# Turning the gate logits of an attention and mixture-of-experts kernel to token rows: 24 small products replaced by three transposes

## The chip, the cores and the metric

The kernel runs on one core of a Trainium2 chip. The metric is the device time of one execution in microseconds; for the kernel before, three runs are known. The engines are called PE (TensorE matmuls), PEld (its weight loads), DVE (VectorE), ACT (ScalarE), POOL (GpSimd) and SP (the queue that issues the transfers).

## The reference

Attention with a window and sink tokens gives 1536 rows of 512 numbers; a dense two-layer block follows, and then eight experts weighted by a gate. The change touches the gate only:

```python
def _moe2_ref(x, w_gate, w1, w2):
    N, D = x.shape                      # 1536, 512
    E = w_gate.shape[1]                 # 8
    logits = x @ w_gate
    logits = logits - logits.max()
    P = np.exp(logits)
    for _ in range(8):
        P /= P.sum(1, keepdims=True) + 1e-09
        P /= P.sum(0, keepdims=True) + 1e-09
        P *= N / E
    out = np.zeros((N, D), dtype=np.float32)
    for e in range(E):
        h = np.maximum(x @ w1[e], 0.0)
        ye = h @ w2[e]
        out += P[:, e:e + 1] * ye
    return out
```

## The kernel before

Attention is computed first. From then on PE works through units. A unit `u` is a pair `(p, c)`: 256 hidden features `p` of a layer and one half `c` of the tokens (768 of 1536). Its first matrix product is done in seven block products `i = 0..6` (`product`, L686) of six matmuls with 384 columns each, because every operand is held as a high and a low part. Products 0, 2, 4 and 5 gather in a PSUM tile `pa`, products 1, 3 and 6 in `pb`. `post` takes them away: ACT copies `pa` to a tile `m` after products 0, 2 and 4 (L693), DVE adds `pb` to it (L699, L708), and ACT and DVE write the high and low part of `h` (L655, L656). A later product into the same `pa` has to wait until that copy has read it.

The second layer of unit `u - 1` is spread over unit `u` as tiles `y` (`l2tile`, L733: six matmuls of 512 columns, three PSUM buffers). They are added to the sum `acc` by DVE (L743, L745) or, for the first feature pair of the experts, copied by ACT (L741).

The order of all this is written out by hand. Step `s = 7u + i` is product `i` of unit `u`, and small jobs hang on steps in three lists: `pre` (before the product), `mid` (after `post`) and `aft` (after the `y` tiles of the step). Each engine takes its instructions in the order in which they were written; a waiting instruction holds up all that stands behind it on its engine.

The gate's logits are computed in units 17 to 19. `gate_split` (POOL, step 112) writes the gate weights as 96 columns `gs`: eight with the high parts, eight with the low parts, zeros. `logits(c, half)` (steps 122, 126, 130, 134) multiplies them with a quarter of the tokens, 384 columns, into the PSUM tile `lps`; ACT copies the 16 rows that matter to a tile `m` (L767). The logits then lie as 16 rows by 384 tokens. `logits_out` (three `mid` steps after each) turns 128 tokens at a time to token rows, and adds the high and low part on the way, with one fp32 product with the 16x8 matrix `pick` (L773), which PE runs as two matmuls. So there are four quarters, 12 products and 24 matmuls. After every third, ACT copies 24 columns to `pr`, 128 tokens by 12 groups by 8 experts (L776).

Then `max_rows`, `max_flip` and `max_exp` find the largest logit and take the exponential, and eight rounds follow of `sink_rows` (five DVE instructions, L793 to L797), `sink_sum` (a product with ones on PE, `cps`, L801) and `sink_cols` (four DVE instructions, L804 to L807). A round takes three steps: `sink_sum` stands two steps behind `sink_rows`, and `sink_cols` one step behind that. Meanwhile `x_fast` prepares the experts' input for the second half of the tokens, on ACT (L267), DVE (L270) and, for two subtractions of 768 columns, POOL (L231); POOL also splits the coming weights (L174, L175).

Of the kernel before, what the change touches and what calls it, by code (L numbers as in the profile page):

```python
# [7 lines left out]
F32 = mybir.dt.float32  # L8
# [3 lines left out]
AF = mybir.ActivationFunctionType  # L12
ALU = mybir.AluOpType
# [3 lines left out]
P = 128  # L17
# [23 lines left out]
def attention_moe_sinkhorn_kernel(  # L41
# [14 lines left out]
    nc = tc.nc  # L56
    B, H, S, D = q.shape
    NTOK, DM = out.shape
    NE, _, FE = w1.shape
    KD = DM // P  # L60
    NQ = S // P
    TH = S // 2
    TQ = S // P
# [6 lines left out]
    pools = {}  # L70
    for nm, bufs in (("const", 1), ("xp", 1), ("stage", 3), ("conv", 2), ("convs", 1), ("wg1", 2), ("wg2", 2), ("ws", 1)):
        pools[nm] = ctx.enter_context(tc.tile_pool(name=nm, bufs=bufs))
    const, xp = pools["const"], pools["xp"]

    ident = const.tile([P, P], F32, name="ident")
# [4 lines left out]
    wide = const.tile([P, 5], F32, name="wide")  # L80
    flag = const.tile([P, 1], I32, name="flag")
    gate = const.tile([P, KD, NE], F32, name="gate")
    pick = const.tile([2 * NE, NE], F32, name="pick")
    X = [xp.tile([P, 7, 2, 2, TH], F32R, name="x0"), None]
    acc = [None, xp.tile([P, KD * S], F32, name="acc1")]

# [235 lines left out]

    def load_gate():
        nc.sync.dma_start(out=gate, in_=w_gate.rearrange("(k p) e -> p k e", p=P))
        nc.vector.tensor_tensor(pick, ident[0:2 * NE, 0:NE], ident[0:2 * NE, NE:2 * NE], op=ALU.add)

    def attention(first):
        with ExitStack() as es:
# [171 lines left out]
            for m in range(NU + 2):  # L500
# [34 lines left out]
                if m == 0:  # L535
                    load_pair(2, "qk")
                    load_pair(1, "v")
                    load_gate()
# [75 lines left out]
    def moe(again):  # L614
        with ExitStack() as es:
            def pool(nm, bufs, **kw):
                return es.enter_context(tc.tile_pool(name=nm, bufs=bufs, reuse_waits="tile", **kw))

            hp, tp, ep = (pool(nm, n, side="right") for nm, n in (("hp", 6), ("mt", 4), ("ep", 3)))
# [53 lines left out]
            unit = {}  # L673
# [76 lines left out]
            mb = [None]  # L750
# [8 lines left out]
            def logits(c, half):  # L759
                g = unit["g"]  # L760
                ps = ps_m.tile([96, TH], F32, tag="m", name="lps")
                seq = [(i, j, k) for i, j in (((0, 0), (1, 2)), ((3, 0), (0, 0), (6, 2)))[half] for k in range(2)]
                seq = [(i, a, j, k) for a in range(2) for i, j, k in seq]
                for n, (i, a, j, k) in enumerate(seq):
                    nc.tensor.matmul(ps, lhsT=g[:, j + k], rhs=X[c][:, i, a, k], start=(n == 0), stop=(n == len(seq) - 1))  # L765
                l = tp.tile([P, TH], F32, tag="m", name="m")
                nc.scalar.activation(l[0:2 * NE], ps[0:2 * NE], AF.Copy)  # L767
                unit["l"] = l

            def logits_out(c, half, t):  # L770
                if t == 0:
                    mb[0] = ps_m.tile([P, TQ // 2, NE], F32, tag="m", name="lpt")
                nc.tensor.matmul(mb[0][:, t], lhsT=unit["l"][0:2 * NE, t * P:(t + 1) * P], rhs=pick)  # L773
                if t == TQ // 2 - 1:
                    r = c * TQ + half * (TQ // 2)
                    nc.scalar.activation(pr[:, r:r + TQ // 2], mb[0], AF.Copy)  # L776

            def max_rows():
                nc.vector.tensor_reduce(lmax[:, 0:1], pr.rearrange("p t e -> p (t e)"), axis=AX.X, op=ALU.max)
# [46 lines left out]
            pre, mid, aft = {}, {}, {}  # L826

            def at(d, i, fn, *args):
                d.setdefault(i, []).append(lambda: fn(*args))
# [41 lines left out]
            i = 7 * U + 10  # L871
            for c in range(2):
                for half in range(2):
                    at(mid, i, logits, c, half)
                    for t in range(TQ // 2):
                        at(mid, i + 1 + t, logits_out, c, half, t)
                    i += 4
            at(pre, i, max_rows)
            at(mid, i + 1, max_flip)
            at(pre, i + 2, max_exp)  # L880
# [5 lines left out]
            i = max(i + 4, 14 * (NPX + NPE))  # L886
# [48 lines left out]
            for t in tiles:  # L935
                t()

    first = moe(False)
    attention(first)
    masks[0] = None  # L940
    for _ in first:
        pass
    with tc.If(nc.values_load(flag[0:1, 0:1], min_val=0, max_val=4 * P) > 0):
        general_attention()
        for _ in moe(True):
            pass
# [31 lines left out]
```

## Time and profile before

| | |
|---|---|
| runs of the kernel before | 1443.67, 1445.56, 1445.78 us, median 1445.56 |
| profiled execution, its own time | 1445.62 us |
| its span, first to last instruction | 1443.8 us |
| PE busy | 1411.7 us, 98% |
| DVE, POOL, ACT busy | 61%, 49%, 36% |
| chain that ended last | PE 88%, DVE 7%, ACT 2%, POOL 2% |

The page gives the busy time of each engine, and the chain of work that ended last by engine and line. The timeline of one engine gives the start of each group of like instructions. A matmul's busy time overlaps the next one's, so what a group costs PE is the distance from its start to the next group's start, not its busy time.

### The profile page before, as it was taken

The numbers are of one execution on the slowest core, as the hardware profiler recorded it, in microseconds if no ns is written. First come the engines' busy times: TensorE is split into PE (matmuls) and PEld (weight loads), VectorE is DVE, ScalarE is ACT, GpSimd is POOL, SyncE is SP. The second block draws the span as 40 slices with busy tenths as digits, with TensorE's granted clock in tenths as the row PEclk, the third lists the DMA queues.
The fourth block names the chain that finished last, engine by engine and source line by source line (L and its number), as shares of the span: only waits on it lengthen the run. The fifth ranks groups of instructions, "written<-read, shape, count | busy, mean of one in ns | idle before, by whom it ended". The sixth has DMA issues, their size and how long they took to land.

```text
span 1443.8 us, 19897 instructions
## 1 busy us (share of the span) xinstructions
PE 1411.7 (98%) x7531; PEld 1279.7 (89%) x7531; DVE 881.2 (61%) x1626; ACT 524.9 (36%) x1151; POOL 714.5 (49%) x843
## 2 busy tenths in 40 slices
PE   7899999999999999999999999999999999999998
PEld 5788889999988888898899889889889889988987
DVE  6877677777784485555555555555555555555544
ACT  5777677667543312222222222222222222222221
POOL 4789745446583446543345444335544334544410
PEclk9999999999999999999999999999999999999999
DMA  7342112112010000110001001000101000100002
GB/s 155 87 87 39 45 59 74 59 63 84 30 59 15 30 30 30 44 44 30 30 30 42 32 30 45 30 30 30 44 30 44 30 30 30 43 31 30 15 1 90
DMA packets 76633, 64.30 MB, mean 45 GB/s; under 512 B 40176, under 2 KB 64752, under 8 KB 76528
## 3 DMA queue, kind: packets, MB, share of 16 engines
q1 hardware_dynamic: 76240, 62.94, 14.7%
q8 instruction: 61, 1.00, 0.3%
q14 instruction: 44, 0.36, 0.1%
q10 hardware_dynamic: 288, 0.00, 0.0%
HBM read 59.79 MB, written 3.15 MB: 44 GB/s over the span
## 4 chain that ended last, share of the span: by engine, by line
PE 88%; DVE 7%; ACT 2%; POOL 2%; issue 1%; DMA 0%; DVEq 0%; ACTq 0%; POOLq 0%
PE y L733 43%; PE pa L686 21%; PE pb L686 16%; PE po L468 3%; PE sps L414 2%; PE xps L450 1%; DVE x L270 1%; PE tps L397 1%; DVE acc L743 1%; PE lps L765 0%; DVE ptB L458 0%; DVE cg L162 0%; ACT h L665 0%; DVE h L667 0%; POOL wg L175 0%
## 5 line engine op out<-in xcount | busy, mean ns | idle before, releaser
L733 PE MATMUL y<-w2s,h 128*128 128x512 f32 x2304 | 584.5, 394 | 0.0
L733 PEld LDWEIGHTS y<-w2s,h 128*128 128x128 f32 x2304 | 427.2, 188 | 72.6
L745 DVE SCALAR_TENSOR_TENSOR acc<-y,pr,acc 128x512 f32<-128x512 f32 x336 | 252.3, 751 | 325.5 <-PE y L733 324.1
L686 PE MATMUL pa<-x,wg 128*128 128x384 f32 x1920 | 387.8, 336 | 2.2 <-ACT m L693 2.0
L686 PEld LDWEIGHTS pa<-x,wg 128*128 128x128 f32 x1920 | 342.2, 188 | 26.1 <-ACT m L693 2.5
L686 PE MATMUL pb<-x,wg 128*128 128x384 f32 x1440 | 290.0, 335 | 3.1 <-DVE h L667 2.7
L693 ACT ACTIVATE m<-pa 128x384 f32<-128x384 f32 x240 | 117.7, 490 | 436.6 <-PE pa L686 436.3
L686 PEld LDWEIGHTS pb<-x,wg 128*128 128x128 f32 x1440 | 253.6, 188 | 10.3 <-DVE h L667 2.0
L174 POOL TENSOR_SCALAR w2s<-raw 128x512 fp32r<-128x512 f32 x64 | 49.0, 765 | 389.8 <-PE y L733 389.8
L655 ACT ACTIVATE h<-m 128x384 fp32r<-128x384 f32 x192 | 100.9, 526 | 295.6 <-DVE m L708 252.2
L733 PE MATMUL y<-h,w2s 128*128 128x384 f32 x768 | 146.9, 335 | 2.8 <-ACT cs L143 1.9
L656 DVE SCALAR_TENSOR_TENSOR h<-m,h 128x384 fp32r<-128x384 f32 x192 | 139.4, 726 | 1.0 <-ACT h L655 0.8
L733 PEld LDWEIGHTS y<-h,w2s 128*128 128x128 f32 x768 | 134.2, 188 | 3.7 <-POOL w2s L174 2.3
L175 POOL TENSOR_TENSOR wg<-raw,wg 128x512 fp32r<-128x512 f32 (+1 forms) x96 | 114.1, 1188 | 8.0
L743 DVE TENSOR_TENSOR acc<-y,acc 128x384 f32<-128x384 f32 (+1 forms) x148 | 84.2, 584 | 39.0 <-PE y L733 38.5
L174 POOL TENSOR_SCALAR wg<-raw 128x512 fp32r<-128x512 f32 (+1 forms) x96 | 54.6, 569 | 97.7 <-PE pa L686 82.8
L708 DVE TENSOR_TENSOR m<-m,pb 128x384 f32<-128x384 f32 x128 | 70.3, 549 | 28.8 <-PE pb L686 28.8
L699 DVE TENSOR_TENSOR m<-m,pb 128x384 f32<-128x384 f32 x80 | 44.2, 553 | 71.3 <-ACT m L693 71.1
L175 POOL TENSOR_TENSOR w2s<-raw,w2s 128x512 fp32r<-128x512 f32 x64 | 84.5, 1320 | 5.3
L175 POOL TENSOR_TENSOR wg<-ws,wg 128x512 fp32r<-128x512 f32 x40 | 54.0, 1350 | 3.3
L655 ACT ACTIVATE h<-pa 128x384 fp32r<-128x384 f32 x64 | 31.5, 492 | 47.7 <-PE pa L686 47.6
L414 PE MATMUL sps<-tk,tq 64*128 64x288 f32 (+2 forms) x288 | 38.3, 358 | 4.3 <-DVE nmax L420 4.3
(141 smaller groups left out, 1298.9 us busy)
## 6 DMA issues: line engine op xcount, KB each, us to landing
raw<-in_moe_w_dram SPq DMA_DIRECT2D x64, 512.0 KB, 3.4
raw<-in_moe_w_in_dram SPq DMA_DIRECT2D x16, 512.0 KB, 3.9
raw<-in_moe_w_out_dram SPq DMA_DIRECT2D x16, 512.0 KB, 3.2
qn<-in_q_dram SPq DMA_DIRECT2D x16, 192.0 KB, 4.0
kn<-in_k_dram SPq DMA_DIRECT2D x16, 192.0 KB, 4.4
vn<-in_v_dram SPq DMA_DIRECT2D x16, 192.0 KB, 3.3
out_dram<-acc SPq DMA_DIRECT2D x12, 256.0 KB, 2.1
par<-in_n_sink_dram ACTq DMA_DIRECT2D x1, 1.0 KB, 2.9
```

The lines of the kernel that those rows point to most:

```text
L174: nc.gpsimd.tensor_scalar(hi, r, 1.0, 1.0, op0=ALU.mult, op1=ALU.mult)
L175: nc.gpsimd.tensor_tensor(lo, r, r32(hi), op=ALU.subtract)
L414: nc.tensor.matmul(ps[:, :b - a], lhsT=x[r, t * P:(t + 1) * P], rhs=y[r, a:b], start=(w == 0), stop=(w == 2))
L655: nc.scalar.activation(h[:, 0], c, AF.Relu)
L656: later.append(lambda: nc.vector.scalar_tensor_tensor(h[:, 1], c, 0.0, r32(h[:, 0]), op0=ALU.max, op1=ALU.subtract))
L686: nc.tensor.matmul(d, lhsT=w[:, s, k], rhs=x[:, t, k], start=(n == 0 and i in (0, 1, 3)), stop=(n == len(seq) - 1), skip_group_check=i in ...
L693: nc.scalar.activation(m, a, AF.Copy)
L699: nc.vector.tensor_tensor(m, m, b, op=ALU.add)
L708: nc.vector.tensor_tensor(c, m, b, op=ALU.add)
L733: nc.tensor.matmul(y, lhsT=lhsT, rhs=rhs, start=(i == 0), stop=(i == len(seq) - 1))
L743: nc.vector.tensor_tensor(o, y, o, op=ALU.add)
L745: nc.vector.scalar_tensor_tensor(o, y, pr[:, c * TQ + tt, e:e + 1], o, op0=ALU.mult, op1=ALU.add)
```

## The change

The tile `pick`, and the DVE instruction that made it, are gone. The four quarters' 16 rows are no longer copied to a tile each: the first takes a buffer of the pool `convw`, which the weights of the layer before have left, POOL fills 384 of its columns with zeros, and quarter `i` is copied by ACT to partitions `32 i` to `32 i + 15`. One step after the last quarter three transposes of 128x128 (the names `lpt<-ident,cg`) turn all of it to token rows; ACT copies the high parts to `pr`, and DVE adds the low parts. `max_rows` and all that follows of the gate stands one step earlier; `weigh_first` stays at step 168.

```diff
-    pick = const.tile([2 * NE, NE], F32, name="pick")
...
-        nc.vector.tensor_tensor(pick, ident[0:2 * NE, 0:NE], ident[0:2 * NE, NE:2 * NE], op=ALU.add)
...
-                l = tp.tile([P, TH], F32, tag="m", name="m")
-                nc.scalar.activation(l[0:2 * NE], ps[0:2 * NE], AF.Copy)
-                unit["l"] = l
-
-            def logits_out(c, half, t):
-                if t == 0:
-                    mb[0] = ps_m.tile([P, TQ // 2, NE], F32, tag="m", name="lpt")
-                nc.tensor.matmul(mb[0][:, t], lhsT=unit["l"][0:2 * NE, t * P:(t + 1) * P], rhs=pick)
-                if t == TQ // 2 - 1:
-                    r = c * TQ + half * (TQ // 2)
-                    nc.scalar.activation(pr[:, r:r + TQ // 2], mb[0], AF.Copy)
+                i = 2 * c + half
+                if i == 0:
+                    unit["l"] = pools["convw"].tile([P, DM], F32, tag="g", name="cg")
+                    nc.gpsimd.memset(unit["l"][:, 0:TH], 0.0)
+                nc.scalar.activation(unit["l"][32 * i:32 * i + 2 * NE, 0:TH], ps[0:2 * NE], AF.Copy)
+
+            def logits_out():
+                lt = ps_m.tile([P, TQ // 2, 4, 32], F32, tag="m", name="lpt")
+                l = unit.pop("l")
+                for t in range(TQ // 2):
+                    nc.tensor.transpose(lt[:, t].rearrange("p i r -> p (i r)"), l[:, t * P:(t + 1) * P], ident)
+                o = pr.rearrange("p (i t) e -> p t i e", i=4)
+                nc.scalar.activation(o, lt[:, :, :, 0:NE], AF.Copy)
+                nc.vector.tensor_tensor(o, lt[:, :, :, NE:2 * NE], o, op=ALU.add)
...
                     at(mid, i, logits, c, half)
-                    for t in range(TQ // 2):
-                        at(mid, i + 1 + t, logits_out, c, half, t)
                     i += 4
+            i -= 1
+            at(mid, i - 2, logits_out)
             at(pre, i, max_rows)
```

On PE, at the last quarter (steps 134 to 138), the rows before:

```order
L765 MATMUL lps<-x_2382,gs 96x384 x12
L733 MATMUL y<-w2s,h 128x512 x6
L686 MATMUL pa<-x_2382,wg_5016 128x384 x6
L773 MATMUL lpt<-pick,m 128x8
L686 MATMUL pb<-x_2382,wg_5065 128x384 x6
L773 MATMUL lpt<-pick,m 128x8
L733 MATMUL y<-w2s,h 128x512 x12
```

and now:

```order
L763 MATMUL lps<-x_2380,gs 96x384 x12
L731 MATMUL y<-w2s,h 128x512 x6
L684 MATMUL pa<-x_2380,wg_5014 128x384 x6
L774 MATMUL lpt<-ident,cg 128x128 x3
L684 MATMUL pb<-x_2380,wg_5063 128x384 x6
L731 MATMUL y<-w2s,h 128x512 x12
```

The small products between the large ones are gone (a row here is one product, which the trace shows as two matmuls), and three transposes stand together.

On POOL, at the first quarter (step 122; `acc` are the two subtractions of `x_fast`), the rows now:

```order
L173 TENSOR_SCALAR w2s<-raw 128x512
L174 TENSOR_TENSOR w2s<-raw,w2s 128x512
L230 TENSOR_TENSOR acc_90<-acc_90 128x2x384
L767 MEMSET cg 128x384
L230 TENSOR_TENSOR acc_90<-acc_90 128x2x384
```

Before, the two subtractions stood together; the filling with zeros now stands between them.

On ACT, from the same step on, with what each row waits for, the rows before:

```order
L693 ACTIVATE m<-pa 128x384 [waits PE_49,Activation_49]
L767 ACTIVATE m<-lps 16x384 [waits PE_49,Activation_49]
L741 ACTIVATE acc_2383<-y 128x512 [waits PE_49] x2
L267 ACTIVATE x_2382<-acc_91 128x768 [waits DVE_49]
L693 ACTIVATE m<-pa 128x384 [waits PE_49,Activation_49]
```

and now:

```order
L691 ACTIVATE m<-pa 128x384 [waits PE_49,Activation_49]
L768 ACTIVATE cg<-lps 16x384 [waits PE_49,Pool_49]
L739 ACTIVATE acc_2381<-y 128x512 [waits PE_49] x2
L266 ACTIVATE x_2380<-acc_90 128x768 [waits DVE_49]
L691 ACTIVATE m<-pa 128x384 [waits PE_49,Activation_49]
```

The copy of the first quarter's logits now also waits for POOL, with the same four instructions behind it.

## Rows read from the trace of the kernel before

**Rows 1.** The page, busy time and share of each engine.

```profile
PE 1411.7 (98%) x7531; PEld 1279.7 (89%) x7531; DVE 881.2 (61%) x1626; ACT 524.9 (36%) x1151; POOL 714.5 (49%) x843
```

**Rows 2.** Timeline of PE at the logits: start us, us, engine line op.

```profile
436.05 1.22 PE L686 MATMUL pa<-x,wg 128*128 128x384 f32 x6
437.21 0.38 PE L773 MATMUL lpt<-pick,m 16*128 16x8 f32 x2
...
444.93 1.22 PE L686 MATMUL pa<-x,wg 128*128 128x384 f32 x6
...
474.02 0.38 PE L773 MATMUL lpt<-pick,m 16*128 16x8 f32 x2
```

**Rows 3.** Timeline of PE after the gate, with large products alone.

```profile
552.94 1.21 PE L686 MATMUL pa<-x,wg 128*128 128x384 f32 x6
553.99 1.20 PE L686 MATMUL pb<-x,wg 128*128 128x384 f32 x6
555.03 1.55 PE L733 MATMUL y<-w2s,h 128*128 128x512 f32 x6
556.41 1.21 PE L686 MATMUL pa<-x,wg 128*128 128x384 f32 x6
```

**Rows 4.** Tile lpt: weight loads (ns min/median/max), and idle time before them.

```profile
L773 PEld LDWEIGHTS lpt<-pick,m x24: 181/182/184, 437.2 to 480.0; 16*128 16x128 f32 x24
...
  issue: 3.0, 12
```

**Rows 5.** Timeline of PE at the transpose that the kernel has already.

```profile
484.17 1.21 PE L686 MATMUL pb<-x,wg 128*128 128x384 f32 x6
485.21 0.27 PE L785 MATMUL mps<-ident,m 128*128 128x128 f32 x1
...
486.72 1.20 PE L686 MATMUL pa<-x,wg 128*128 128x384 f32 x6
```

**Rows 6.** Timeline of PE at a product with ones of the eight rounds.

```profile
541.61 1.20 PE L686 MATMUL pb<-x,wg 128*128 128x384 f32 x6
542.65 0.28 PE L801 MATMUL cps<-cpart,ones 128*128 128x8 f32 x2
...
545.62 1.23 PE L686 MATMUL pa<-x,wg 128*128 128x384 f32 x6
```

**Rows 7.** Timeline of POOL at the first quarter; in brackets the idle time before and its releaser.

```profile
434.53 3.63 POOL L231 TENSOR_TENSOR acc<-acc 128x768 f32<-128x768 f32 x2 [4.96 <-DVE x L270]
```

**Rows 8.** Tile gs: the zero filling of another tile by POOL.

```profile
L755 POOL MEMSET gs<- x1: 412/412/412, 418.5 to 418.5; 128x384 f32 x1
```

**Rows 9.** Timeline of ACT at the first quarter, and at the last quarter's copy.

```profile
433.55 0.48 ACT L767 ACTIVATE m<-lps 16x384 f32<-16x384 f32 x1 [0.81 <-PE lps L765]
...
436.25 0.60 ACT L741 ACTIVATE acc<-y 128x512 f32<-128x512 f32 x1 [0.77 <-PE y L733]
436.75 0.83 ACT L267 ACTIVATE x<-acc 128x768 fp32r<-128x768 f32 x1
437.48 0.48 ACT L693 ACTIVATE m<-pa 128x384 f32<-128x384 f32 x1
...
471.75 0.48 ACT L767 ACTIVATE m<-lps 16x384 f32<-16x384 f32 x1 [1.00 <-PE lps L765]
```

**Rows 10.** Timeline of PE during the eight rounds: the groups it waited for.

```profile
500.59 1.32 PE L686 MATMUL pb<-x,wg 128*128 128x384 f32 x6 [0.29 <-DVE m L699]
...
522.38 0.39 PE L801 MATMUL cps<-cpart,ones 128*128 128x8 f32 x2 [0.42 <-DVE cpart L797]
...
524.39 1.28 PE L686 MATMUL pa<-x,wg 128*128 128x384 f32 x6 [0.16 <-ACT m L693]
```

**Rows 11.** Timeline of DVE: first and last of one round's nine instructions.

```profile
504.15 0.15 DVE L804 TENSOR_SCALAR cinv<-cps 128x8 f32<-128x8 f32 x1
...
507.61 0.36 DVE L797 TENSOR_REDUCE cpart<-pr 128x8 f32<-128x96 f32 x1
```

**Rows 12.** Timeline of DVE ahead of max_rows.

```profile
480.60 0.55 DVE L699 TENSOR_TENSOR m<-m,pb 128x384 f32<-128x384 f32 x1 [9.26 <-ACT m L693]
```

## The prediction

> **What bounds the kernel now.** I read the page first. PE is busy for 98% of the span and no other engine for more than 61% [rows 1], so what PE is spared counts, unless PE then waits for something else. Next I read PE's timeline at the logits, to see what the small products cost in their place. Large products alone follow each other at fixed distances: 1.05 us from a `pa` or `pb` group to the next, 1.38 us from a `y` group to the next [rows 3]. Whatever lies beyond these distances is the price of what stands between. Last I read ACT and POOL at the first quarter, because the change lets an ACT instruction wait for POOL there, and DVE in the eight rounds, which the change moves by a step.
>
> **Removed: 12 products, 24 matmuls.** From the `pa` of step 123 to the `pa` of step 126 PE takes 444.93 - 436.05 = 8.88 us [rows 2]. In it lie three groups of 1.05, three of 1.38 and three small products. The large groups alone would take 3 x (1.05 + 1.38) = 7.29, so a small product costs 0.53 us. The other three quarters give the same within 0.02 us, by the same reckoning. Twelve cost 12 x 0.53 = 6.4 us, all on PE's path, since PE runs without a gap here. The busy times hide that: two matmuls of eight columns look like 0.38 us, most of it overlapped. The trace shows where the price comes from: each of the 12 pairs has some 0.25 us in which the weight load stands idle for "issue" (3.0 us in 12 cases), and then two loads of 0.18 us [rows 4].
>
> Removing the four ACT copies to `pr` and the one small DVE instruction that makes `pick` gains nothing: neither is what PE waits for.
>
> **Added on PE: three transposes.** One transpose of the same shape is there already: from `pb` to `pa` around it PE takes 486.72 - 484.17 = 2.55 us, against 1.05 + 1.38 = 2.43 without [rows 5]. That is 0.12 to 0.13 us each, 0.4 us for three. They wait for the last quarter's copy, which starts at 471.75 and takes 0.48 us [rows 9], while their place is where a small product starts at 474.02 [rows 2]: 1.8 us to spare, so no wait. The Trainium skill ("TensorE: Matmul & The Clock Gate", Part 4) speaks against cheap transposes: about 0.275 us each in a kernel. By that figure the three would cost 0.8 us, and the sum would come out 0.4 us worse; the row above has the measured price among neighbours, so I keep 0.4.
>
> **Added on ACT and DVE behind the transposes.** ACT copies to `pr` and DVE adds. DVE stood idle for 9.26 us before its instruction at 480.60 [rows 12], so the addition, and `max_rows` behind it, lie in that gap. Cost on PE's path: none. Were the cover gone, it would be one DVE instruction of at most the 0.55 us that a wider one takes there.
>
> **Added: a wait of ACT for POOL.** The zero filling stands on POOL between the two subtractions, as its order shows, and the first of these starts only at 434.53, released by DVE; the two take 3.63 us, so the first ends at about 436.35 [rows 7]. A filling of the same 128x384 takes 0.41 us [rows 8]. So the first quarter's copy, which ran at 433.55 [rows 9], now starts at about 436.8. Behind it on ACT stand two copies of `y` (0.50 us from start to start), one of `x` (0.73) and the copy of `pa` after product 4 [rows 9]. That copy then ends at 436.8 + 0.48 + 2 x 0.50 + 0.73 + 0.48 = 439.5, where it ended at 437.96 before. Product 5 writes into the same `pa` and has to wait for it. Without the small product it would start at 436.05 + 1.05 + 1.38 = 438.5. **PE waits 1.0 us.** Nothing worse follows: the next `y` groups have three buffers, the addition on DVE behind that copy (0.55 us) ends two PE groups before product 6 needs it, and ACT, idle before several rows here, catches up within the unit. Bounds: 0 if the filling came early, 1.5 if ACT's spacing is looser than these rows. The later three quarters wait for PE alone, as before.
>
> **Moved: `max_rows` and the eight rounds, one step earlier.** No instruction is added, but each round's nine DVE instructions, 3.8 us while POOL works beside them (504.15 to 507.97) [rows 11], meet other neighbours. Before, PE waited 0.29 + 0.42 + 0.16 = 0.87 us for this stage [rows 10]. Now other rounds stand ahead of the additions that free `pb` and of `h`; one of them, at step 146, stands right ahead of the low part of `h` that PE needs two steps on. I take the same total, so 0; the ends are a gain of 0.9, all of the old waits, and a loss of 2.1, two groups of 1.05 us by which a late round could hold PE. `weigh_first` stays where it was, so the rounds' earlier end moves nothing behind them. SP issues the same transfers.
>
> **The sum.** -6.4 + 0.4 + 1.0 + 0 = -5.0 us. The profiled execution took 1445.62 us, its span 1443.8 with 1.8 around it; that is 0.06 above the median of the runs. So I forecast **1440.6 us**, 0.35% less. A measurement of this kernel can tell about 0.2%, 2.9 us, from no change: below 1442.7 counts as faster.
>
> **Rivals.**
>
> *The wait for POOL isn't felt, or the old waits vanish.* If PE does not wait at product 5, the time is 1439.6; with the 0.87 us of the rounds gone as well, 1438.7. For it: PE has few waits anywhere in this stage. Against: the chain of ACT instructions above has no slack in its sum. 15%.
>
> *The moved rounds cost two more waits* of 1.05 us: 1442.7. For it: a round takes DVE 3.8 us beside POOL, while PE needs only a few groups for three steps, and PE did wait for such a round at 522.38 [rows 10]. Against: just three short waits in eight rounds before. 11%.
>
> *The small products cost only what like ones cost.* The product with ones has two matmuls of eight columns too, and from its `pb` to the `pa` behind it PE takes 4.01 us against 1.05 + 2 x 1.38 = 3.81 [rows 6], 0.2 us for the pair. If the other 0.33 us at `lpt` were not its own but a cost of the place that the transposes or the wait inherit, the change would save 12 x 0.2 = 2.4, and the sum would be -2.4 + 0.4 + 1.0 = -1.0: 1444.6, no change that can be told. The Trainium skill says that a weight load's time goes by its columns and not its rows ("TensorE: Matmul & The Clock Gate", LDWEIGHTS), by which a 16-row operand should cost what a 128-row one costs. The loads agree, 182 ns here [rows 4]; the idle 0.25 us ahead of them does not, and it stands at `lpt` alone. 8%.
>
> *Slower: the rounds fall behind in every step.* If the new places let each of the eight rounds end after PE has reached its product with ones, PE waits about one group, 1.05 us, in each: 8.4 us, against the 0.87 us that go. The sum is -5.0 + 8.4 - 0.9 = +2.5: 1448.1. It decides from about 0.7 us for each round on, where the gain is gone. Against: rounds and products move together and keep their distance of two steps, and DVE is busy for 61% of the span [rows 1]. 4%.
>
> **How the numbers follow.** The forecast keeps 62%, with 1439.8 to 1441.6 as its own range, which takes in a wait between 0.2 and 1.5 us and rounds that differ by half a microsecond. The range to hold 8 times in 10 reaches from the first rival's lower part to beyond the second, 1438.2 to 1443.8; outside lie the third and fourth (12%) and what is unknown. Faster by over 0.2%: 62 + 15 + about half of the second rival, 82%. Within 0.2%: the rest of the second and the third, 14%. Slower: 4%.
>
> **What would show it.** In the changed profile PE should have no group between large products at the first three quarters, with distances of 1.05 and 1.38 us; `lpt` should be three matmuls costing 0.4 us together; ACT's first copy of logits should start near 436.8 after a wait for POOL; and PE should show one wait of about 1 us for ACT's `m` near 438.5. In the eight rounds PE's waits should add up to around 0.9 us. I am wrong if the span from 436 to the first round shrinks by less than 4 us, if PE's waits in the rounds exceed 3 us, or if the time comes back later, for instance as PE waiting for POOL's weights.

## The result and the profile after

The changed kernel takes **1430.81 us** (median of 4 runs, 1428.6 to 1432.42); the kernel before took 1444.62 beside it (4 runs, 1441.36 to 1445.78). The ratio is 0.991, with a 95% interval of 0.9898 to 0.9922. It is faster, as forecast, but by nearly three times the 5.0 us forecast, and it lies below the range. The profiled execution took 1428.6 us, with a span of 1426.8.

The page, busy time by engine, after:

```profile
PE 1393.6 (98%) x7510; PEld 1273.4 (89%) x7510; DVE 884.1 (62%) x1626; ACT 523.8 (37%) x1148; POOL 714.1 (50%) x844
```

PE is busy for 18.1 us less than in [rows 1], with 21 instructions fewer. 21 small matmuls can't be 18 us, so other matmuls must have become shorter. To find them I took the starts of PE's products (a `pa` or `pb` group is one step's product, and both kernels issue the same 560) and compared the two kernels at the same five steps, 51, 101, 121, 181 and 551. Timeline of PE, before (start us, us, engine line op):

```profile
270.95 1.20 PE L686 MATMUL pa<-x,wg 128*128 128x384 f32 x6
...
381.58 1.20 PE L686 MATMUL pb<-x,wg 128*128 128x384 f32 x6
...
429.79 1.21 PE L686 MATMUL pa<-x,wg 128*128 128x384 f32 x6
...
581.79 1.21 PE L686 MATMUL pb<-x,wg 128*128 128x384 f32 x6
...
1408.27 1.21 PE L686 MATMUL pa<-x,wg 128*128 128x384 f32 x6
```

and after:

```profile
267.63 1.22 PE L684 MATMUL pa<-x,wg 128*128 128x384 f32 x6
...
379.33 1.21 PE L684 MATMUL pb<-x,wg 128*128 128x384 f32 x6
...
427.65 1.21 PE L684 MATMUL pa<-x,wg 128*128 128x384 f32 x6
...
572.39 1.21 PE L684 MATMUL pb<-x,wg 128*128 128x384 f32 x6
...
1391.48 1.21 PE L684 MATMUL pa<-x,wg 128*128 128x384 f32 x6
```

| stretch (us) | before | after | difference |
|---|---|---|---|
| start to step 51 (attention, first units) | 270.95 | 267.63 | -3.3 |
| 51 to 101 (dense layer) | 110.63 | 111.70 | +1.1 |
| 101 to 121 | 48.21 | 48.32 | +0.1 |
| 121 to 181 (gate, with the edit) | 152.00 | 144.74 | -7.3 |
| 181 to 551 (experts) | 826.48 | 819.09 | -7.4 |
| 551 to the end of the span | 35.53 | 35.32 | -0.2 |

The first row says nothing of the edit. `e4_fill_early`, `e15_noacc_d32` and `e13_rounds_old`, described below, run the changed kernel's instructions at its addresses up to step 51, and reach it at 271.95, 269.30 and 272.37 us. One cause is the granted clock: from 120 to 148 us it is 0.94 before and 1.00 after (column PEclk, third from the right, of the windows view; before first):

```profile
120.00:148.00 28.00, 26.27 (x200) 23.25 (x197) 19.25 (x65) 20.21 (x65) 23.48 (x34) 0.94 0.07 15
```

```profile
120.00:148.00 28.00, 25.30 (x198) 22.38 (x195) 18.91 (x62) 19.28 (x60) 23.61 (x39) 1.00 0.07 16
```

The 0.94 is a mean: from about 142.1 to 145.5 us the clock stood at 0.50, the lower of its two levels (1.2 GHz), and otherwise at the upper one (2.4 GHz). Just before, up to 140.79 us, PE had waited 1.19 us for DVE. Fifteen matmuls of 128x384 took 3.65 us from 141.76 on, and fifteen like them 2.20 us from 145.59 on, so this stay explains about 1.5 of the 3.3 us; the rest stays open. Because single runs differ by such amounts ahead of step 51, what follows goes by stretches behind it.

The rest adds up to -13.7 us, and the medians differ by 13.8. Only half of that stands where the code was edited. The other half is in the experts, where neither instructions nor order changed and PE waits for nothing in either kernel. Timeline of PE there, before and after:

```profile
1203.57 1.55 PE L733 MATMUL y<-w2s,h 128*128 128x512 f32 x6
1204.95 1.21 PE L686 MATMUL pa<-x,wg 128*128 128x384 f32 x6
```

```profile
1204.11 1.53 PE L731 MATMUL y<-w2s,h 128*128 128x512 f32 x6
1205.48 1.21 PE L684 MATMUL pa<-x,wg 128*128 128x384 f32 x6
```

A `y` group of six matmuls takes PE 1.37 us instead of 1.38 to 1.39, start to start. Added up from start to start, the 317 `y` groups of this stretch take 433.32 us instead of 439.44, the 211 `pa` groups 220.15 instead of 221.46, and the 159 `pb` groups 165.6 in both: that is the 7.4 us. In the dense layer it goes the other way: `pa` (303.38) to `y` (304.44) takes 1.06 after, where [rows 3] and the dense layer before (302.15 to 303.19) show 1.04 to 1.05.

```profile
302.15 1.20 PE L686 MATMUL pa<-x,wg 128*128 128x384 f32 x6
303.19 1.20 PE L686 MATMUL pb<-x,wg 128*128 128x384 f32 x6
```

```profile
303.38 1.22 PE L684 MATMUL pa<-x,wg 128*128 128x384 f32 x6
304.44 1.22 PE L731 MATMUL y<-h,w2s 128*128 128x384 f32 x6
```

What differs all over the program is where tiles lie. `pick` took 32 bytes of every partition. Without it, each tile allocated behind it at the lower end of SBUF (`x`, `acc`, `raw`, `cg`, `wg1`, `wg2`, `ws`, `pr`) lies 32 bytes lower: the first `x` at 18624 instead of 18656, `acc` at 61632 instead of 61664, by the allocation of the two built programs. The tiles at the upper end (`w2s`, `h`, `m`, `e`, `wg3`) stay. Below, the *difference* is the upper addresses minus the lower ones, modulo 128 bytes: 0 before, 32 after. The 128 is a way of counting; no run moved tiles by 128 bytes alone to see whether that changes nothing.

### The profile page after: what moved, and what is told of

It is laid out like the page before. It is cut to its first block, busy times and chain, and to the rows that moved or that the text cites. A ratio compares the mean times of both kernels' runs of the same rounds, so it can differ in the third digit from the quotient of the medians.

```text
span 1426.8 us, 19856 instructions
## 1 busy us (share of the span) xinstructions
PE 1393.6 (98%) x7510; PEld 1273.4 (89%) x7510; DVE 884.1 (62%) x1626; ACT 523.8 (37%) x1148; POOL 714.1 (50%) x844
## 4 chain that ended last, share of the span: by engine, by line
PE 88%; DVE 7%; ACT 2%; POOL 1%; issue 1%; DMA 0%; DVEq 0%; POOLq 0%; ACTq 0%
PE y L731 43%; PE pa L684 22%; PE pb L684 16%; PE po L466 3%; PE sps L412 2%; PE xps L448 1%; DVE x L269 1%; PE tps L395 1%; DVE acc L741 1%; DVE ptB L456 0%; DVE h L665 0%; ACT h L663 0%; DVE cg L161 0%; PE lps L763 0%; DVE cs L159 0%
## 5 line engine op out<-in xcount | busy, mean ns | idle before, releaser
L731 PE MATMUL y<-w2s,h 128*128 128x512 f32 x2304 | 576.3, 390 | 0.0
```

Source lines behind the costliest of these rows:

```text
L731: nc.tensor.matmul(y, lhsT=lhsT, rhs=rhs, start=(i == 0), stop=(i == len(seq) - 1))
```

## The experiments

The theory: the experts' gain comes from the addresses, and the edit's own work is worth about what was forecast. The rival: it comes from the edit's order and waits, which reach further than the sum said.

**Addresses put back, and moved alone.** `e1_pad_after` is the changed kernel with a dead tile in the place of `pick` (difference 0). `e2_pad_before` is the kernel before with a second one (96).

```diff
+    const.tile([2 * NE, NE], F32, name="pad")
```

> The changed kernel with an unused tile of 32 bytes per partition in the place of pick, so that every tile stands at the address it had before the change (x, acc, the weights of the first layer at 32 modulo 64 bytes); the instructions are those of the changed kernel. Theory A (addresses): the 32 bytes that pick gave up moved the tiles behind it, and that made the y groups of the experts quicker (1.39 to 1.37 us) and the groups of the dense layer slower (1.04 to 1.06). Then this kernel has the old distances again and takes about 1437 us, near my forecast of 1440.6. Theory B (the gate's own instructions made the rest quicker, or the runs differ by chance): 1431 us and y groups of 1.37.

> The kernel before with 32 unused bytes more behind pick, so that x, acc and the first layer's weights stand at 0 modulo 64 bytes as in the changed kernel; the instructions are those of before. Theory A: y groups of the experts at 1.37 us, dense layer at 1.06, and about 1444.6 - 7.8 + 1.7 = 1438.5 us. Theory B: 1444.6 us and 1.39.

`e1_pad_after` took 1439.98 us (5 runs) against 1446.12 of the kernel before (14 runs), a ratio of 0.9951 (0.9932 to 0.9971); `e2_pad_before` 1442.91, a ratio of 0.9988 (0.9974 to 1.0002), not told apart from no change. In `e1_pad_after` the experts are slow again, from 573.06 to 1399.55 or 826.49 us, and the `y` group takes 1.39:

```profile
573.06 1.21 PE L685 MATMUL pb<-x,wg 128*128 128x384 f32 x6
...
1210.48 1.55 PE L732 MATMUL y<-w2s,h 128*128 128x512 f32 x6
1211.87 1.21 PE L685 MATMUL pa<-x,wg 128*128 128x384 f32 x6
...
1399.55 1.20 PE L685 MATMUL pa<-x,wg 128*128 128x384 f32 x6
```

So the experts' gain is the addresses' and not the order's; the rival falls. The gate stretch is 145.75 here, against 152.00 before at the same addresses: **the edit itself gives 6.25 us**. In `e2_pad_before` the experts take 823.68 and the dense layer 111.83 (before 110.63). The 1438.5 us that theory A gave for it were missed: its `y` groups do fall to 434.17 us in all, but its `pa` and `pb` groups rise from 387.0 to 389.5, so another shift is no gain of the same size.

**Both ends moved.** `e3_right` moves the upper tiles of the changed kernel by 32 bytes too, so that the difference is 0 at new places; `e8_d64` moves them by 96 (difference 64; the tile has 24 columns instead of `NE`).

```diff
+            pool("rpad", 1, side="right").tile([P, NE], F32, name="rpad")
```

> The changed kernel with 32 unused bytes at the other end of SBUF, so that w2s, h, m and e stand at 0 modulo 64 bytes too, like all else. If what counts is each tile's own place in 64 bytes, at least as fast as the changed kernel, 1431 us or less, and y groups of 1.37 or less. If what counts is whether the two ends agree, the state of before is back in this respect (both were at 32): y groups of 1.39 and about 1437 us. Theory B: 1431 us.

> The changed kernel with 96 unused bytes at the other end of SBUF: the two ends then differ by 64 modulo 128 bytes, after 0 (e1, e3: y 1.39, dense layer 1.04), 32 (the changed kernel: 1.37, 1.06) and 96 (e2: 1.37, 1.06). If only the difference modulo 64 counts, as 64-byte lines would have it, the distances of e1 and e3 come back, 1.39 and 1.04, and about 1438 us; if it counts modulo 128, another pair of distances.

`e3_right`: 1437.31 us, a ratio of 0.9938 (0.9917 to 0.9959), experts 826.48, `y` group 1.39:

```profile
1211.41 1.55 PE L732 MATMUL y<-w2s,h 128*128 128x512 f32 x6
1212.80 1.21 PE L685 MATMUL pa<-x,wg 128*128 128x384 f32 x6
```

The relation between the two ends counts, not the place of either, as far as this shift of both by 32 bytes shows. In the traces that share a difference the experts' stretch repeats to the hundredth: 826.48 or 826.49 at 0 (before, `e1_pad_after`, `e3_right`, `e14_noacc_d0`), 819.09 at 32 (after, `e4_fill_early`, `e13_rounds_old`, `e15_noacc_d32`). So one trace is enough to tell such stretches apart. `e8_d64`: 1432.13 in one run, experts 819.80. So it isn't a matter of 64 bytes either: 0 and 64 differ by 6.7 us. By differences of 0, 32, 64 and 96 (in bytes moved, upper end against lower: 0, +32, -64, -32) the experts take 826.48, 819.09, 819.80 and 823.68 us. The time that PE spends in the `y` matmuls of the whole program is, before and after (groups of PE's lines; columns: busy us and mean ns of one, idle us before):

```profile
L733 PE MATMUL y<-w2s,h 128*128 128x512 f32 x2304 | 584.5, 394 | 0.0
```

```profile
L731 PE MATMUL y<-w2s,h 128*128 128x512 f32 x2304 | 576.3, 390 | 0.0
```

In `e8_d64` it is 578.2 us.

**The filling with zeros earlier.** `e4_fill_early` leaves everything of the change but fills one step before the first quarter, ahead of the subtractions.

```diff
+            def fill_logits():
+                unit["l"] = pools["convw"].tile([P, DM], F32, tag="g", name="cg")
+                nc.gpsimd.memset(unit["l"][:, 0:TH], 0.0)
...
+            at(aft, i - 1, fill_logits)
```

> The changed kernel with the zero filling one step earlier, ahead of both subtractions on POOL, which is idle there. PE's wait for the copy m near 437 (0.8 us; 0.96 by the distance of the groups) goes and nothing else changes: 0.8 to 1.0 us less than the changed kernel, about 1430. If that wait only hid another one behind it, no difference.

The filling runs at 431.67 and PE no longer waits (timeline of PE):

```profile
438.17 1.21 PE L684 MATMUL pa<-x,wg 128*128 128x384 f32 x6
439.21 1.53 PE L731 MATMUL y<-w2s,h 128*128 128x512 f32 x6
440.58 1.21 PE L684 MATMUL pa<-x,wg 128*128 128x384 f32 x6
```

The gate stretch falls from 144.74 to 143.69, by 1.05 us. In the total this can't be told: 1432.22 us (4 runs), a ratio of 0.9894 (0.9865 to 0.9922) to the kernel before. It is a better version by the stretch alone.

**The rounds at their old step.** `e13_rounds_old` keeps the products and transposes of the change but puts the rounds back.

```diff
-            i -= 1
-            at(mid, i - 2, logits_out)
+            at(mid, i - 3, logits_out)
```

> The changed kernel with max_rows and the eight rounds back at their old steps (one later); the transposes stay where they are. My forecast had the move at 0, with ends of a gain of 0.9 and a loss of 2.1 us. If the move took PE's waits in the rounds away, they come back here: 0.9 us by the profile's brackets (up to 1.5 by the distances of the groups), and the stretch from the first logits to the end of the rounds is longer by that. If the waits went because the small products went, no wait here either.

It took 1434.82 us in one run. The gate stretch becomes 146.18, 1.44 us longer, and two waits for DVE are back. The changed kernel has a single wait of PE from 420 to 575 us, the one for ACT at the first quarter (waits of PE: total us, times, longest):

```profile
PE pa L684 <- ACT m L691: 0.8, 1, 0.8
```

The two waits in the timeline of PE of `e13_rounds_old`, and between them the same groups without a wait (511.77 to 514.42):

```profile
495.95 1.52 PE L731 MATMUL y<-w2s,h 128*128 128x512 f32 x6
497.80 1.31 PE L684 MATMUL pb<-x,wg 128*128 128x384 f32 x6 [0.32 <-DVE m L697]
...
511.77 1.21 PE L684 MATMUL pa<-x,wg 128*128 128x384 f32 x6
...
514.42 1.22 PE L684 MATMUL pb<-x,wg 128*128 128x384 f32 x6
...
517.89 1.21 PE L684 MATMUL pb<-x,wg 128*128 128x384 f32 x6
519.57 0.39 PE L802 MATMUL cps<-cpart,ones 128*128 128x8 f32 x2 [0.48 <-DVE cpart L798]
...
521.59 1.28 PE L684 MATMUL pa<-x,wg 128*128 128x384 f32 x6
```

The brackets show 0.32 and 0.48 us of idle time, but the distances show more. From `y` to `pb` at the first wait PE takes 1.85 us where 1.37 is usual, so 0.48. At the second it takes 3.70 us from a product over `cps` and `y` to the next product, against 2.65, so 1.05. Together these are 1.5 us, about the 1.44 of the stretch. A bracket begins where the last matmul ends. It leaves out the overlap that is lost (the `y` group at 495.95 is busy for 1.52 us, and the next group usually starts after 1.37) and the slower groups behind the wait.

**Which tiles meet.** From `e1_pad_after` (difference 0), one set of tiles at a time is moved by 96 bytes, which is 32 the other way modulo 128, with a dead tile of 24 columns ahead and one of 8 behind. The tiles behind both dead tiles then move by 128 bytes, and keep their place only by the count modulo 128. The sets are `acc`, `x`, and `wg1` with `wg2` at the lower end; `w2s`, `h`, `m` with `e`, and `wg3` at the upper. The edit for `w2s` as an example:

```diff
+            pool("rpad0", 1, side="right").tile([P, 24], F32, name="rpad0")
...
+            pool("rpad1", 1, side="right").tile([P, 8], F32, name="rpad1")
```

> The changed kernel with all tiles at their old addresses as in e1, but the two tiles acc alone moved by 32 bytes down modulo 128 (padding before and behind them). If the quicker y groups come from DVE's reading and writing of acc beside PE's reading of w2s and h at the other end of SBUF, the y groups of the experts go to 1.37 us here and the rest stays at the old distances (dense layer 1.04). If acc has no part in it, all distances are those of e1: 1.39 and 1.04.

> As e5, but with the two tiles x moved alone, and acc at its old place. If PE's own reading of x is what meets w2s, h or wg3, the distances of y (1.39) or of the dense layer's groups (1.04) change here: to 1.37, or to 1.06. If not: 1.39 and 1.04.

> As e5, but with the weight tiles wg1 and wg2 of the first layer moved alone. If it is PE's weight loads of the next product groups (wg) during the last matmuls of a y group (which stream w2s) that cost, y groups go to 1.37 us here, and the dense layer's groups perhaps to 1.06. If not: 1.39 and 1.04.

> The changed kernel with all tiles at the old addresses as in e1, and the tiles w2s alone moved by 32 bytes up modulo 128. w2s is what PE streams in the experts' second layer, beside weight loads from h. If the pair w2s and h sets the y distance, it changes here and in e10 (from 1.39 to 1.37), while the changed kernel, which kept both together, could not have gained by it. If it is w2s against everything at the other end (x, wg, acc), y goes to 1.37 here as in the changed kernel, and the first layer's groups stay at 1.04.

> As e9 with the tiles h alone moved. y at 1.37 if h is what counts (PE loads it as weights, ACT and DVE write it); 1.39 if not.

> As e9 with the tiles m and e alone moved, which PE never reads: ACT and DVE write and read them. If PE's distances depend only on what PE reads, 1.39 and 1.04 as in e1. If the other engines' traffic counts, as e5 (acc alone: first-layer groups 1.06 in place of 1.04) has it, a change here too.

> As e9 with the tiles wg3 alone moved: the weights of products 3 and 6 (in pb), which lie at the other end from x and were apart from it in the changed kernel. If that pair counts, the distances from pb groups change here; the y distance of 1.39 stays.

| moved | time, one run | experts 181 to 551 | of it `y` | of it `pa` and `pb` | dense 51 to 101 |
|---|---|---|---|---|---|
| nothing (`e1_pad_after`) | 1439.98 (median) | 826.49 | 439.4 | 387.0 | 110.62 |
| `acc` (e5) | 1437.65 | 827.91 | 436.8 | 391.1 | 111.27 |
| `x` (e6) | 1442.55 | 827.35 | 436.7 | 390.7 | 111.46 |
| `wg1`, `wg2` (e7) | 1438.19 | 826.85 | 437.0 | 389.8 | 111.28 |
| `w2s` (e9) | 1446.11 | 832.49 | 443.7 | 388.8 | 111.82 |
| `h` (e10) | 1442.02 | 830.00 | 442.6 | 387.4 | 111.98 |
| `m`, `e` (e11) | 1446.57 | 831.07 | 442.0 | 389.0 | 111.81 |
| `wg3` (e12) | 1438.86 | 828.25 | 439.2 | 389.1 | 110.93 |

No set alone brings the gain, and each costs something in the experts, 0.4 to 6.0 us; the totals of one run don't show that. In none of them does a `y` group go to 1.37, and only e12 leaves the `y` groups as they were, so the cases written ahead for e5 to e11 decide little. Moves at the lower end shorten the `y` groups by 2.4 to 2.8 us in all and lengthen the `pa` and `pb` groups by 2.8 to 4.0; moves of `w2s`, `h` or `m` with `e` lengthen the `y` groups by 2.6 to 4.2. Only e12 came as written: `y` stays, and the `pb` groups, where `wg3` is read, rise from 165.6 to 167.6 us. It is also the only one of these runs in which no other tile moves, by the allocation of the built programs. In e11, for instance, `w2s` and `wg3` move by 128 bytes behind `m` and `e`. So e11 would show that tiles count which PE doesn't read in the experts only if 128 bytes made no difference, and no run tested that.

**Without DVE's weighted additions.** These 751 ns instructions stream `y` and `acc` all through the experts. `e14_noacc_d0` (from `e1_pad_after`, 1439.60 us in one run) and `e15_noacc_d32` (from the change, 1430.41) leave out 324 of them, so their output lacks these terms.

```diff
-                else:
+                elif p == NP - 1:
```

> The kernel of e1 (all tiles at their old addresses, y distance 1.39 us), leaving out DVE's weighted additions of y to acc for experts 1 to 7 (but for the last feature pair's). If what slows PE in the y groups at these addresses is DVE's traffic on acc, they go to the level that the kernel without additions has at the changed addresses too (e15), below 1.39. If PE's own reads set the distance, 1.39 stays.

> The changed kernel (y distance 1.37 us), leaving out the same additions. If acc's traffic is the cause of the difference, the same distance as e14; if PE's own reads or the traffic of ACT and DVE on m and h are, still 0.02 us less than e14.

The experts take 826.49 and 819.09 us, to the hundredth what they take with the additions. A `y` group takes 1.39 and 1.37 us. PE in `e14_noacc_d0`:

```profile
1202.46 1.55 PE L732 MATMUL y<-w2s,h 128*128 128x512 f32 x6
1203.85 1.20 PE L685 MATMUL pa<-x,wg 128*128 128x384 f32 x6
```

So these additions are not what PE meets at either difference. Between steps 181 and 551 they are all that touches `acc`, and yet `e5_acc` changed PE's pace there. That suggests that in e5 the 128 bytes count by which the tiles behind `acc` move, and not `acc` itself, but no run shows it. Which streams meet stays open.

## Why the prediction was wrong, step by step

**The step that failed** is the sentence that removing the copies to `pr` and "the one small DVE instruction that makes `pick` gains nothing". It counted what the instruction did and not what the tile held. Giving back 32 bytes per partition moved half of the program's tiles, and that is worth -7.4 us in the experts, -1.0 in the gate stretch (145.75 to 144.74) and some +1.2 ahead of it. The sum put the addresses at nothing without a reason, and no rival or bound had them. With the addresses held, `e1_pad_after` lies at 1439.98, within the range and 0.6 from the forecast; by the ratio it gains 7.1 us, with an interval of 4.2 to 9.8. That it comes so near is in part luck: its runs spread from 1434.82 to 1441.31, and the stretch shows 6.25 us of gain where the forecast had 5.0.

**The steps at the edit**, 6.25 us by `e1_pad_after`:

- *Products, -6.4: right.* Large groups now follow each other at 1.04 to 1.05 and 1.37 us with nothing between, where a small product stood in each place [rows 2]. With the other three terms as measured below, the 6.25 us leave 6.2 for the products. Timeline of PE at the first quarter, after:

```profile
433.86 1.21 PE L684 MATMUL pa<-x,wg 128*128 128x384 f32 x6
434.90 1.52 PE L731 MATMUL y<-w2s,h 128*128 128x512 f32 x6
437.23 1.31 PE L684 MATMUL pa<-x,wg 128*128 128x384 f32 x6 [0.80 <-ACT m L691]
438.38 1.52 PE L731 MATMUL y<-w2s,h 128*128 128x512 f32 x6
439.74 1.21 PE L684 MATMUL pb<-x,wg 128*128 128x384 f32 x6
440.78 1.53 PE L731 MATMUL y<-w2s,h 128*128 128x512 f32 x6
442.15 1.21 PE L684 MATMUL pa<-x,wg 128*128 128x384 f32 x6
```

- *ACT's wait for POOL, +1.0: right.* From 433.86 to 442.15 PE takes 8.29 us; three groups of 1.05 and three of 1.37 are 7.26, so 1.03 is the wait, shown as 0.80 idle and slower groups around it. `e4_fill_early` gives back 1.05. The chain runs as I had it, 2.2 us earlier as everything there (433.86 against 436.05 in [rows 2]): filling at 434.18 behind the first subtraction, copy of the logits at 434.63 after a wait for POOL, where [rows 9] had a wait for PE (timelines of POOL, then ACT):

```profile
434.18 0.42 POOL L767 MEMSET cg<- 128x384 f32 x1
```

```profile
434.63 0.48 ACT L768 ACTIVATE cg<-lps 16x384 f32<-16x384 f32 x1 [4.03 <-POOL cg L767]
435.02 1.05 ACT L739 ACTIVATE acc<-y 128x512 f32<-128x512 f32 x2
435.98 0.83 ACT L266 ACTIVATE x<-acc 128x768 fp32r<-128x768 f32 x1
436.71 0.46 ACT L691 ACTIVATE m<-pa 128x384 f32<-128x384 f32 x1
```

- *Transposes, +0.4: right.* Timeline of PE at the last quarter:

```profile
466.67 1.21 PE L684 MATMUL pa<-x,wg 128*128 128x384 f32 x6
467.72 0.49 PE L774 MATMUL lpt<-ident,cg 128*128 128x128 f32 x3
467.96 1.30 PE L684 MATMUL pb<-x,wg 128*128 128x384 f32 x6
469.11 2.89 PE L731 MATMUL y<-w2s,h 128*128 128x512 f32 x12
```

  From `pa` to `y` PE takes 469.11 - 466.67 = 2.44 us; two groups of 1.05 are 2.10, so the three cost 0.34. The 0.8 us estimated from the figure of the Trainium skill ("TensorE: Matmul & The Clock Gate", Part 4: about 275 ns each in one kernel's context) is not what they cost PE. As a duration the figure agrees, 272 ns for each here; overlap hides more than half of it.
- *Moved rounds, 0: mis-sized.* `e13_rounds_old` puts them at -1.44 us, beyond the gain of 0.9 that I gave as an end. The old waits for DVE [rows 10] vanish, as in the lower part of the first rival. I had priced them by the idle time in the brackets, 0.87; by the distances the two waits of `e13_rounds_old` cost 1.5, with 0.80 in their brackets. For the products I had gone by the distances, and there the price was right.

These terms sum to -6.4 + 0.34 + 1.03 - 1.44 = -6.5; the stretch shows -6.25. Of the rivals, half of the first came out: the wait for POOL is felt, and the old waits are gone. The others are out: no round makes PE wait, the move gave time instead of costing two groups, and the products gave about 6.2 us and not 2.4.

## What to carry to other kernels

An edit that frees or adds bytes in on-chip memory moves every tile behind it, and this kernel, which TensorE bounds, gained half a per cent by that in a stage that was never edited. Compare the distances between like groups in an untouched stage; if they changed, put a dead tile in the freed place, and measure the edit with it. What such a shift gives is no merit of the edit and may go with the next one: try a few paddings at the end, on their own. And price a wait by the distance between the groups around it: the idle time in the brackets was about half of what the waits in the rounds cost.

## What the runs showed of the hardware

- PE's pace depends on where the tiles of the two ends of SBUF lie to each other: a `y` group of six 128x512 products takes 1.39 us at a difference of 0 modulo 128 bytes and 1.37 at 32, and the experts take 826.48, 819.09, 819.80 and 823.68 us at 0, 32, 64 and 96. The dense layer goes the other way: 110.63, 111.70, 111.75, 111.83. All shifts were multiples of 32 bytes. The Trainium skill ("SBUF — State Buffer", Specifications) tells of 16-byte lines, with a penalty for each cross to a new one. No shift here changes where a tile starts in such a line, so that rule gives no difference between these kernels, and the measurement shows up to 7.4 us.
- Moving `wg3` alone by 96 bytes adds 1.8 us to the experts, in the `pb` groups. Taking out 324 additions on `acc` changes nothing, to the hundredth of a microsecond.
